# Products with v in one group per head: an order of work rearranged in a kernel for hashed attention and soft mixture of experts

## The chip, the core and the metric

The kernel runs on one core of one Trainium2 chip. A core has five engines that each work through their own instructions in the order in which the program wrote them: TensorE (PE in the profile; PEld is its loading of weights), VectorE (DVE), ScalarE (ACT), GpSimd (POOL) and SyncE (SP), which here only issues transfers. The metric is the time of one execution on the device in microseconds (us), lower is better. Times are medians of several runs; a profile comes from one execution.

## What is computed

There are 4 batches of 8 heads, 768 positions, 64 dimensions a head.

```python
q_bits = (np.einsum('bhsd,dk->bhsk', q, proj) > 0)      # 6 bits, and the same for k
mask = q_bucket[:, :, :, None] == k_bucket[:, :, None, :]
scores = scale * np.matmul(q, k.transpose(0, 1, 3, 2))
scores = np.where(mask, scores, -1000000000.0)
scores = scores - np.max(scores, axis=-1, keepdims=True)
attn = np.exp(scores)
attn = attn / (np.sum(attn, axis=-1, keepdims=True) + 1e-09)
attn_out = np.matmul(attn, v)
...
x = attn_out.transpose(0, 2, 1, 3).reshape(3072, 512)
logits = x @ phi                                        # 32 slots
d = softmax of logits over the 3072 rows; slot_input = d.T @ x
h = np.maximum(slot_input[e] @ w1[e], 0.0); slot_out[e] = h @ w2[e]   # 8 experts
c = softmax of logits over the 32 slots; return c @ slot_out
```

## The kernel before, in words

Heads are worked on in pairs, an even one and the odd one behind it, because q and k of two heads fill the 128 partitions together. Four things overlap: loading and splitting the next pair, the maxima of the next head, the scores of this head, and the sums of the last pair.

For a pair, `bits` (line 322) multiplies q and k with the projection on TensorE, in column tiles of 32 (several small products side by side in the array), and VectorE thresholds the result (line 319) into `bt`. ScalarE writes rounded high parts of q and k into `w4` (`split_hi`, line 279), and `split_lo` (line 288) subtracts them from the originals to get the low parts. The `spread` functions copy all this into the operands X and Y of the two heads, by transfers that SyncE issues from line 294.

For a head, `smax` (line 358) makes the masked scores once in order to take the row maxima: 12 calls, in PSUM tiles of which there are two, each emptied by a VectorE reduction (lines 371 and 374). `shift` (line 376, VectorE) turns the maxima into a shift, and `shift_rows` (line 387) transposes it on TensorE (line 402), copies it on ScalarE (line 405) and sends it into a row of X and Y. `scores` (line 409) makes the scores a second time, now shifted, transposed, in full-width matmuls (line 419), and ScalarE takes the exponential into the three buffers `pts` (line 423). Each of the buffers holds two of a head's six row tiles. `acc` (line 425) adds a buffer into a running sum on GpSimd (lines 430, 436), `av` (line 438) multiplies it with v on TensorE in two column tiles of 64 (line 447). The third `av` of a head is followed by a copy on ScalarE (line 451, `avs`).

For a pair that is through, `pair_sum` (line 454) adds the partitions of the running sums on TensorE in column tiles of 32 (line 459), and ScalarE copies the result to `sm` (line 462). `pair_log` (line 468) multiplies the heads' outputs with phi in row and column tiles (line 474). `pair_turn` (line 490) transposes the sums (line 494), after which VectorE copies and inverts them (lines 496, 497), `pair_rec` (line 464) inverts `sm` in three pieces on VectorE (line 466), `pair_add` (line 478) adds the scaled logits into `lacc` (lines 486, 488), and `pair_x` (line 499) transposes the outputs and scales them into `xq` (lines 509, 511).

At the end of a batch, `batch_max` and the functions behind it fold the logits' halves together (lines 605, 606, VectorE), take maxima and exponentials, transpose them (line 636), multiply them with `xq` (line 653) and rescale the running results. The experts' layers come after all heads.

The order is written by hand. `WHEN` gives each call a due time in slots (six slots a head), `FIRST` overrides single calls, `at` collects them, and the plan is sorted by due time; the calls are then made in that order, and every engine gets its instructions in that order. A call of two engines (a matmul and the reduction of its result) stands at the same place in both. Waits are semaphores put in for the buffers and operands. `p_mi`, the PSUM pool of the sums, logits, bits and transposes, has two tiles, the pool of the scores has three, `raw`, `w4` and `bt` have one each.

In an even head the order around line 494 is, before: the turn, two of the reciprocals, av 1 and the logits, the first scores of the odd head, a maximum, av 2.

Of the kernel before, what the change touches and what calls it, by code (L numbers as in the profile page):

```python
# [12 lines left out]
ALU = mybir.AluOpType  # L13
# [32 lines left out]
 'bits': -14.465,  # L46
 'split_hi': -14.035,
 'split_lo': [-13.1, -12.626],
# [19 lines left out]
 'batch_scale': 24.396,  # L68
 'batch_slots': 26.173,
 'batch_combine': 24.296,  # L70
 'load_weights': 4.18}

FIRST = {('load', 4): 4.476,
 ('bits', 2): 1.288,
# [71 lines left out]
def lsh_attention_soft_moe(  # L146
# [141 lines left out]
    def split_lo(h, x):  # L288
        w = st[h]["w4"]
        (nc.vector if h else nc.gpsimd).tensor_tensor(out=w[:, 2 * x + 1], in0=st[h]["raw"][:, x], in1=w[:, 2 * x], op=ALU.subtract)  # L290
# [308 lines left out]

    def batch_max(b):  # L600
        z = bst[b]
        if "dl" not in z:
            lacc = lacc_of[b]
            dl = z["dl"] = dp.tile([P, HC], F32, name="dl", bufs=1)
            nc.vector.tensor_copy(dl[0:64], lacc[64:128])
            nc.vector.tensor_tensor(out=dl[64:128], in0=lacc[0:64], in1=dl[0:64], op=ALU.add)  # L606
# [16 lines left out]
    def batch_scale(b):  # L623
        z = bst[b]
        if b == 0:
            nc.vector.tensor_copy(run_l, z["lb"])
        else:
            nc.vector.tensor_copy(z["al"][64:128], z["al"][0:64])
            nc.vector.scalar_tensor_tensor(out=run_l, in0=run_l, scalar=z["al"][0:2 * NS], in1=z["lb"],
                                           op0=ALU.mult, op1=ALU.add)  # L630
# [55 lines left out]
    def batch_combine(b):  # L686
        z = bst[b]
        lg = z["tm"][:, :, 1]
        m = dp.tile([P, 3, 2], F32, name="cm", bufs=1)
        sm = dp.tile([P, 3, 2], F32, name="cs", bufs=1)  # L690
        cb = call[:, b]
        nc.vector.tensor_reduce(out=m, in_=lg, axis=AX.X, op=ALU.max)
        nc.vector.tensor_tensor(out=cb, in0=lg, in1=m[:, :, :, None].broadcast_to([P, 3, 2, NS]), op=ALU.subtract)
        nc.scalar.activation(cb, cb, AF.Exp)
# [3 lines left out]
        nc.vector.tensor_tensor(out=cb, in0=cb, in1=sm[:, :, :, None].broadcast_to([P, 3, 2, NS]), op=ALU.mult)  # L698
# [17 lines left out]
    for h in range(BH):  # L716
# [16 lines left out]
        for j in range(NT // 2):  # L733
# [5 lines left out]
            else:  # L739
                at(s0 + WHEN["av"][x][j], av, h, j)  # L740
# [10 lines left out]
        if h % H == H - 1 and h < BH - 1:  # L751
            for f in (batch_max, batch_exp, batch_turn, batch_scale, batch_slots, batch_combine):
                at(p0 + WHEN[f.__name__], f, h // H)
# [72 lines left out]
    batch_combine(B - 1)  # L826
# [170 lines left out]
```

## Time and profile before

| | |
|---|---|
| median of 3 runs | 537.56 us (537.41 to 540.1) |
| the profiled execution | 537.24 us |
| its span from first to last instruction | 535.4 us |
| granted TensorE clock, mean | 0.972 |
| busy: PE, PEld | 503.6, 286.7 us |
| busy: DVE, ACT, POOL | 388.9, 246.6, 317.9 us |
| instructions | 9102 |

An engine's busy time is the time in which it worked on some instruction. In the rows of the profile an operation is named by its engine, its line in the kernel, what it writes and reads, its shape, and how often it came. "L368 <- DVE mx L374" behind a time says that the instruction waited that long and that the named one ended the wait. Matmuls are pipelined: the next one starts before the recorded end of the last, so distances between starts tell more than durations.

### The profile page before, as it was taken

What the parts mean: (1) busy time and instruction counts of PE and PEld (TensorE: products, weight loads), DVE (VectorE), ACT (ScalarE), POOL (GpSimd) and SP (SyncE); (2) the same over time, 40 slices, a digit from 0 to 9 for tenths busy, and PEclk for the clock granted to TensorE, in tenths of its full rate; (3) what the DMA queues carried; (4) which work ended last, traced back from release to release, by engine and by line L of the source; (5) the groups of instructions that cost most, each with busy time, mean ns of one, the idle gap of its engine ahead of it and who ended that gap; (6) DMA issues with size and microseconds to landing.
All of it is one profiled execution on the core that took longest, in us unless ns stands there. A gap on an engine that the chain in (4) does not pass through costs nothing.

```text
span 535.4 us, 9102 instructions
## 1 busy us (share of the span) xinstructions
PE 503.6 (94%) x3164; PEld 286.7 (54%) x3164; DVE 388.9 (73%) x717; ACT 246.6 (46%) x460; POOL 317.9 (59%) x210
## 2 busy tenths in 40 slices
PE   6979999999989999999989999999899999999992
PEld 4544555655545565656544555565445656553562
DVE  6475777888898777877898788686997875465233
ACT  4145455545453454545453545454534555422232
POOL 9256858585854576767646585858635767511200
PEclk9789999999998999999989999999999999999997
DMA  4766566757673667676753757676626366888976
GB/s 123 184 137 152 173 174 187 186 174 183 175 179 95 177 180 180 179 178 178 185 163 98 184 176 179 187 180 190 130 76 144 77 150 217 296 314 330 409 284 275
DMA packets 39778, 99.60 MB, mean 186 GB/s; under 512 B 7458, under 2 KB 13732, under 8 KB 39732
## 3 DMA queue, kind: packets, MB, share of 16 engines
q1 hardware_dynamic: 39540, 98.94, 64.7%
q8 instruction: 25, 0.41, 0.3%
q14 instruction: 21, 0.17, 0.1%
q0 software_dynamic: 192, 0.08, 0.1%
HBM read 52.76 MB, written 6.29 MB: 110 GB/s over the span
## 4 chain that ended last, share of the span: by engine, by line
PE 71%; DVE 17%; DMA 4%; SPq 3%; issue 2%; ACT 1%; DVEq 0%; ACTq 0%
PE av L447 20%; PE st L419 20%; PE smx L368 12%; DVE mx L374 4%; DVE w L290 4%; SPq L294 3%; PE qs L920 3%; PE qh L838 3%; PE mi L459 2%; PE mi L474 2%; DVE mx L371 2%; PE mi L326 1%; DVE dl L606 1%; DMA XY<-bt 1%; DMA XY<-mr 1%
## 5 line engine op out<-in xcount | busy, mean ns | idle before, releaser
L436 POOL TENSOR_TENSOR acc<-acc,pt 128x768 f32<-128x768 f32 x125 | 236.4, 1891 | 56.2 <-ACT pt L423 45.8
L423 ACT ACTIVATE pt<-st 128x512 f32<-128x512 f32 x288 | 163.1, 595 | 105.1 <-PE st L419 98.2
L419 PE MATMUL st<-XY 128*128 128x512 f32 (+1 forms) x768 | 184.1, 348 | 0.0
L374 DVE TENSOR_REDUCE mx<-smx 128x1 f32<-128x512 f32 x192 | 130.4, 686 | 56.2 <-PE smx L368 55.9
L447 PE MATMUL av<-pt,v 128*64 128x384 f32 x768 | 148.4, 508 | 0.0
L368 PE MATMUL smx<-XY 96*128 96x512 f32 (+1 forms) x384 | 127.3, 378 | 18.0 <-DVE mx L374 14.5
L419 PEld LDWEIGHTS st<-XY 128*128 128x128 f32 x768 | 123.9, 191 | 21.2 <-issue 10.6
L430 POOL TENSOR_TENSOR acc<-pt 128x768 f32<-128x768 f32 x32 | 58.5, 1829 | 98.0 <-ACT pt L423 98.0
L368 PEld LDWEIGHTS smx<-XY 96*128 96x128 f32 x384 | 71.2, 193 | 81.1 <-DVE mx L374 35.9
L447 PEld LDWEIGHTS av<-pt,v 128*64 128x64 f32 x768 | 47.0, 137 | 63.2 <-issue 57.2
L371 DVE TENSOR_REDUCE mx<-smx 128x2 f32<-128x512 f32 x96 | 65.5, 682 | 4.8 <-PE smx L368 4.6
L290 DVE TENSOR_TENSOR w<-raw,w 128x768 fp32r<-128x768 f32 x30 | 41.3, 1377 | 2.9 <-ACT w L286 2.8
L466 DVE RECIPROCAL sm<-sm 128x128 f32<-128x128 f32 x45 | 39.6, 909 | 0.0
L286 ACT CAST w<-raw 128x768 fp32r<-128x768 f32 x32 | 25.1, 830 | 18.6 <-DMA XY<-w 14.1
L451 ACT COPY avs<-av 128x384 f32<-128x384 f32 x32 | 15.3, 479 | 37.3 <-PE av L447 37.2
L405 ACT CAST mr<-mi 12x128 fp32r<-12x128 f32 x31 | 7.9, 254 | 51.1 <-PE mi L402 51.1
L319 DVE TENSOR_SCALAR bt<-mi,con 128x384 fp32r<-128x384 f32 x15 | 10.1, 677 | 18.4 <-PE mi L402 8.8
L511 DVE TENSOR_TENSOR xq<-mi,r 128x256 f32<-128x256 f32 x45 | 17.3, 412 | 0.4 <-PE mi L509 0.4
L920 PE MATMUL qs<-w 128*32 128x256 f32 x232 | 15.2, 382 | 0.0
L509 PE MATMUL mi<-ident,avs 128*128 128x128 f32 x90 | 14.8, 273 | 0.0
L326 PE MATMUL mi<-raw,pb 128*32 128x384 f32 x128 | 14.5, 498 | 0.3 <-DMA raw<-qk 0.2
L838 PE MATMUL qh<-w,siT 128*32 128x512 f32 x128 | 14.6, 595 | 0.0
(169 smaller groups left out, 340.7 us busy)
## 6 DMA issues: line engine op xcount, KB each, us to landing
w<-w SPq DMA_DIRECT2D x61, 512.0 KB
XY<-w SPq DMA_DIRECT2D x63, 384.0 KB
raw<-qk SPq DMA_DIRECT2D x32, 384.0 KB
XY<-w SPq DMA_DIRECT2D x64, 192.0 KB
v<-vt SPq DMA_DIRECT2D x32, 192.0 KB
out<-w SPq DMA_DIRECT2D x12, 512.0 KB
xq<-w SPq DMA_DIRECT2D x3, 512.0 KB
XY<-bt SPq DMA_DIRECT2D x62, 19.5 KB
```

What stands on the lines that cost most here:

```text
L290: (nc.vector if h else nc.gpsimd).tensor_tensor(out=w[:, 2 * x + 1], in0=st[h]["raw"][:, x], in1=w[:, 2 * x], op=ALU.subtract)
L368: nc.tensor.matmul(pt[:, o:o + b - a], s["Y"][0:96, 0, t * P:(t + 1) * P], s["Y"][0:96, 1, a:b], start=True, stop=True)
L371: nc.vector.tensor_reduce(out=mx[:, n - 1:n + 1], in_=pt.rearrange("p (a x) -> p a x", a=2), axis=AX.X, op=ALU.max)
L374: nc.vector.reduce_max(out=mx[:, n:n + 1], in_=pt, axis=AX.X)
L419: nc.tensor.matmul(pt[:, o:o + b - a], x[:, 1, i * P:(i + 1) * P], x[:, 0, a:b], start=first, stop=not first)
L423: nc.scalar.activation(s["P", i // 2][:, 512 * u:512 * u + 512], pt, AF.Exp, scale=D ** -0.5)
L430: nc.gpsimd.tensor_tensor(out=s["acc"], in0=pr[:, 0:S], in1=pr[:, S:2 * S], op=ALU.add)
L436: eng.tensor_tensor(out=s["acc"], in0=s["acc"], in1=pr[:, a * S:(a + 1) * S], op=ALU.add)
L447: nc.tensor.matmul(s["av"][64 * c:64 * c + 64, 0:HC], s["v"][:, i, :], pr[:, o + c * HC:o + (c + 1) * HC], start=(i == 0), stop=(i == NT - 1))
L466: nc.vector.reciprocal(out=rs[:, k * P:(k + 1) * P], in_=rs[:, k * P:(k + 1) * P])
L838: nc.tensor.matmul(ph[fh][32 * j:32 * j + 32], siT[:, k, 4 * g + j, :], wt[0, g, k, j][:, fh * 512:(fh + 1) * 512], start=(k == 0), stop=( ...
L920: nc.tensor.matmul(po[32 * j:32 * j + 32], hTs[g][:, f, 32 * j:32 * j + 32], wt[1, x, 2 * g + f // 4, j][:, (f % 4) * HM:(f % 4 + 1) * HM] ...
```

## The change

No product is added or left out. The due times move, three VectorE steps move to other engines, and two functions are cut in two. In short:

- the three `av` calls of a head stand together behind its last scores; for an even head `pair_sum` and `pair_log` stand ahead of them and `pair_turn` and two pieces of `pair_rec` behind them; for an odd head `bits` stands behind them, `split_hi` and both `split_lo` between them
- `shift_rows` moves later, `pair_x` earlier
- `split_lo` of q runs on GpSimd for all pairs (before: for the first pair alone)
- the fold of the logits' halves becomes `batch_both`, with the copy on ScalarE and the addition on GpSimd, at 20.1 instead of 21.535
- the update of `run_l` and two steps of the combination weights run on GpSimd, for all batches but the last
- the last head's `av` and the first pair's start keep their old times

```diff
- 'bits': -14.465,
- 'split_hi': -14.035,
- 'split_lo': [-13.1, -12.626],
+ 'bits': -12.18,
+ 'split_hi': -12.196,
+ 'split_lo': [-12.193, -12.19],
- 'shift_rows': [-2.151, -1.917],
+ 'shift_rows': [-1.8, -1.1],
- 'av': [[3.513, 6.554, 6.938], [3.513, 5.087, 6.68]],
- 'pair_sum': 16.448,
- 'pair_turn': 18.256,
- 'pair_rec': [18.379, 18.389, 18.942],
- 'pair_log': 18.557,
- 'pair_x': [22.815, 24.33],
+ 'av': [[6.7, 6.71, 6.72], [5.8, 5.81, 5.82]],
+ 'pair_sum': 18.6,
+ 'pair_turn': 18.74,
+ 'pair_rec': [18.75, 18.76, 18.942],
+ 'pair_log': 18.65,
+ 'pair_x': [22.3, 23.0],
- 'batch_max': 21.535,
- 'batch_exp': 22.897,
- 'batch_turn': 23.51,
+ 'batch_both': 20.1,
+ 'batch_max': 22.4,
+ 'batch_exp': 23.0,
+ 'batch_turn': 23.9,
- 'batch_combine': 24.296,
+ 'batch_weigh': 24.65,
+ 'batch_share': 27.6,
...
-        (nc.vector if h else nc.gpsimd).tensor_tensor(out=w[:, 2 * x + 1], ...
+        (nc.vector if h and x else nc.gpsimd).tensor_tensor(out=w[:, 2 * x + 1], ...
...
+    def batch_both(b):
+        lacc = lacc_of[b]
+        dl = bst[b]["dl"] = dp.tile([P, HC], F32, name="dl", bufs=1)
+        nc.scalar.copy(dl[0:64], lacc[64:128])
+        nc.gpsimd.tensor_tensor(out=dl[64:128], in0=lacc[0:64], in1=dl[0:64], op=ALU.add)
...
-            nc.vector.tensor_copy(dl[0:64], lacc[64:128])
-            nc.vector.tensor_tensor(out=dl[64:128], in0=lacc[0:64], in1=dl[0:64], op=ALU.add)
...
+            if b < B - 1:
+                nc.gpsimd.tensor_tensor(out=run_l, in0=run_l, in1=z["al"][0:2 * NS], op=ALU.mult)
+                nc.gpsimd.tensor_tensor(out=run_l, in0=run_l, in1=z["lb"], op=ALU.add)
...
+    def batch_weigh(b):
...
+        eng = nc.gpsimd if b < B - 1 else nc.vector
+        nc.vector.tensor_reduce(out=m, in_=lg, axis=AX.X, op=ALU.max)
+        eng.tensor_tensor(out=cb, in0=lg, in1=m[...].broadcast_to([P, 3, 2, NS]), op=ALU.subtract)
+        nc.scalar.activation(cb, cb, AF.Exp)
+    def batch_share(b):
...
+        nc.vector.reciprocal(out=sm, in_=sm)
+        eng.tensor_tensor(out=cb, in0=cb, in1=sm[...].broadcast_to([P, 3, 2, NS]), op=ALU.mult)
```

More of the change, by code (lines that the diff above doesn't have):

```diff
@@ L289, in split_lo @@
         w = st[h]["w4"]
-        (nc.vector if h else nc.gpsimd).tensor_tensor(out=w[:, 2 * x + 1], in0=st[h]["raw"][:, x], in1=w[:, 2 * x], op=ALU.subtract)
+        (nc.vector if h and x else nc.gpsimd).tensor_tensor(out=w[:, 2 * x + 1], in0=st[h]["raw"][:, x], in1=w[:, 2 * x], op=ALU.subtract)
     def move(dst, src, eng=nc.sync):
@@ L697, in batch_combine @@
         nc.vector.reciprocal(out=sm, in_=sm)
-        nc.vector.tensor_tensor(out=cb, in0=cb, in1=sm[:, :, :, None].broadcast_to([P, 3, 2, NS]), op=ALU.mult)
+        eng.tensor_tensor(out=cb, in0=cb, in1=sm[:, :, :, None].broadcast_to([P, 3, 2, NS]), op=ALU.mult)
     plan = []
@@ L751, in lsh_attention_soft_moe @@
         if h % H == H - 1 and h < BH - 1:
[L752 removed]
+            for f in (batch_both, batch_max, batch_exp, batch_turn, batch_scale, batch_slots, batch_weigh, batch_share):
                 at(p0 + WHEN[f.__name__], f, h // H)
```

28 lines of the change are left out of this document (15 added, 13 removed).

## The prediction

> **What bounds the kernel now.** I read the page first: busy shares, then the chain that ended last.
>
> ```profile
> PE 503.6 (94%) x3164; PEld 286.7 (54%) x3164; DVE 388.9 (73%) x717; ACT 246.6 (46%) x460; POOL 317.9 (59%) x210
> PE 71%; DVE 17%; DMA 4%; SPq 3%; issue 2%; ACT 1%; DVEq 0%; ACTq 0%
> ```
>
> TensorE is busy nearly always, and the chain runs through it; VectorE holds most of the rest. These are averages, so next came the busy time by stretches, each from one pair's sums (line 459) to the next pair's. Columns: length, then busy time of PE, weight loads, DVE, ACT, POOL, and the granted clock.
>
> ```profile
> 254.20:288.80 34.60, 30.70 (x171) 16.65 (x170) 31.49 (x52) 15.38 (x30) 19.39 (x12) 0.95 0.53 139
> 315.40:341.60 26.20, 26.20 (x156) 15.18 (x155) 20.16 (x39) 13.70 (x25) 19.16 (x11) 1.00 0.67 183
> ```
>
> In an ordinary pair TensorE never stops: 26.20 of 26.20 us. A pair with a batch end takes 8.4 us more. So an ordinary pair can only gain if its TensorE work gets cheaper, and any new wait of TensorE adds in full.
>
> **What a group costs.** The timeline of TensorE around one set of products with v, asked in narrow slices so that each start can be read (start, time, operation; a row can run on into the next):
>
> ```profile
> 312.20 0.40 PE L419 MATMUL st<-XY 128*128 128x512 f32 x1
> 312.43 0.39 PE L419 MATMUL st<-XY 128*128 128x512 f32 x1
> 312.75 0.54 PE L447 MATMUL av<-pt,v 128*64 128x384 f32 x2
> 313.12 0.81 PE L447 MATMUL av<-pt,v 128*64 128x384 f32 x4
> 313.77 0.49 PE L447 MATMUL av<-pt,v 128*64 128x384 f32 x2
> 314.19 0.50 PE L368 MATMUL smx<-XY 96*128 96x512 f32 x1
> 314.53 0.28 PE L402 MATMUL mi<-ident,mz 128*12 128x128 f32 x1
> ```
>
> Two 512-column matmuls start 0.23 apart; the second is followed after 0.32 when the tiling changes (+0.09). Two column halves take (313.77 - 313.12) / 2 = 0.325, the first 0.37 (+0.045), the last 0.42 (+0.095); the first full-width matmul afterwards takes 0.34 instead of 0.23 (+0.11). One excursion into column tiles costs 0.34 us.
>
> Before, a pair makes seven: the even head's av 0; the sums; av 1 with the logits; av 2; the odd head's av 0 with the bits; av 1; av 2. After, it makes two: sums, logits, av 0, 1, 2; and av 0, 1, 2, bits. Five fewer save 5 x 0.34 = 1.7; one more change of form inside a group returns about 0.1. **-1.6 us a pair, -24 us over 15 pairs.** The Trainium skill, "TensorEngine Tiling (Array Packing)", section Key Properties, says that changing the tiling mode drains TensorE; the rows above price that drain. By the rule alone the change would be a plain gain, which is the first rival below.
>
> **What the long groups do to VectorE.** TensorE obeys the written order, and so does VectorE. Before, TensorE's order around the turn of the sums (line 494) is:
>
> ```profile
> 317.97 0.49 PE L494 MATMUL mi<-ident,sm 128*128 128x128 f32 x3
> 318.39 1.51 PE L447 MATMUL av<-pt,v 128*64 128x384 f32 x8
> 319.83 0.85 PE L474 MATMUL mi<-avs,phs 64*32 64x384 f32 x8
> 320.61 0.73 PE L419 MATMUL st<-XY 128*128 128x512 f32 x2
> 323.29 0.63 PE L419 MATMUL st<-XY 128*128 128x256 f32 x4
> 323.77 0.28 PE L368 MATMUL smx<-XY 96*128 96x256 f32 x1
> ```
>
> and VectorE's, in the same microseconds:
>
> ```profile
> 319.14 0.16 DVE L496 COPY r<-mi 128x12 f32<-128x12 f32 x1
> 319.34 0.23 DVE L497 RECIPROCAL r<-r 128x12 f32<-128x12 f32 x1
> 319.48 1.71 DVE L466 RECIPROCAL sm<-sm 128x128 f32<-128x128 f32 x2
> 321.62 0.69 DVE L374 TENSOR_REDUCE mx<-smx 128x1 f32<-128x512 f32 x1 [0.43 <-PE smx L368]
> 322.23 0.94 DVE L466 RECIPROCAL sm<-sm 128x128 f32<-128x128 f32 x1
> 324.10 0.55 DVE L486 TENSOR_TENSOR sm<-mi,sm 128x384 f32<-128x384 f32 x1
> 324.68 0.56 DVE L488 TENSOR_TENSOR lacc<-lacc,sm 128x384 f32<-128x384 f32 x1
> 325.16 0.68 DVE L371 TENSOR_REDUCE mx<-smx 128x2 f32<-128x512 f32 x1
> 325.84 0.69 DVE L374 TENSOR_REDUCE mx<-smx 128x1 f32<-128x512 f32 x1
> 326.57 0.17 DVE L380 TENSOR_REDUCE m<-mx 128x6 f32<-128x12 f32 x1
> 326.77 0.38 DVE L381 TENSOR_SCALAR mz<-m 128x6 f32<-128x6 f32 x1
> 327.18 0.17 DVE L383 SCALAR_TENSOR_TENSOR mz<-m,mz 128x6 f32<-128x6 f32 x1
> ```
>
> The two reciprocals run while TensorE does av 1 and the logits, 2.22 us in which it needs nothing of VectorE. Starts follow at 0.61 after a reduction, 0.81 a reciprocal (half of 1.71 with overlap), 0.20 and 0.14 for the two small ones, 0.58 and 0.48 for the additions, 0.68 and 0.73 for the last reductions.
>
> After, the turn comes *behind* the whole group, and VectorE's queue holds the copy of r, hence everything later, until then. Count from the start of the turn. It ends at about 0.6; r's copy starts at 0.65, its reciprocal at 0.85, the long ones at 0.99 and 1.80, the next reduction of the maxima at 2.61, ending at 3.30. TensorE meanwhile does the turn (0.43), one score pair of 512 (2 x 0.23), two maxima of 512 (0.47) and two score pairs of 256 (4 x 0.12), and at 1.85 wants a PSUM buffer for the next maxima. There are two, and that reduction holds one: TensorE stands 1.5 us. VectorE stays the late one: third reciprocal 3.22, reduction 4.03, additions 4.64 and 5.22, reductions 5.70 and 6.38, then the shift (lines 380 to 383) 7.10 to 7.88. The row of shifts (line 402) needs it. Without waits TensorE would be there after five score pairs of 512 (2.34), five of 256 (1.2), four maxima of 512 (0.93), two of 256 (0.24) and the turn: 5.14. **First window: +2.75 us.** Line 381 can also take longer, as here:
>
> ```profile
> 286.63 1.03 DVE L381 TENSOR_SCALAR mz<-m 128x6 f32<-128x6 f32 x1
> ```
>
> Ends: 2.0, if of the waits behind the first 1.5 only half a microsecond is real; 3.4, if line 381 takes its 1.03 each time. A gain is excluded, since nothing leaves VectorE's queue in this window. I take 2.75, every term of which has a row.
>
> **Second window**, behind the odd group, with the bits at its end:
>
> ```profile
> 328.85 0.68 DVE L319 TENSOR_SCALAR bt<-mi,con 128x384 fp32r<-128x384 f32 x1 [1.50 <-PE mi L402]
> 332.50 3.57 SPq L294 DMA_DIRECT2D XY<-bt  x4
> 126.16 2.27 DMA XY<-bt
> ```
>
> VectorE now thresholds the bits (0.68) just as the window opens and its maxima queue behind: TensorE waits 0.5 and 0.1 for buffers. Then the next even head's first maxima need the bits' four rows. The threshold ends at 0.83, the last of four issues starts 3/4 x 3.57 later, and it lands 2.27 after that: 5.8. TensorE would be there at 4.35 (four score pairs of 512, four of 256, four maxima of 512, four of 256, first matmul +0.1): 1.45 late, the 0.6 included. Before, the four issues start at 332.50 in a pair that ends at 341.60, with these maxima among its last work. Another 0.25 goes on the maxima that wait behind the shift. **Second window: +1.7 us** (0.6 if only the buffers count, 2.2 if SyncE's queue is late). Nothing gives these back: the groups last about 5.5 and 4.9 us, and VectorE has only two buffered reductions to do in each.
>
> Every full pair has both windows: 14 x 4.45 = **+62 us**. The last pair has no maxima left.
>
> **Moves that cost nothing or little.** The prices of q's low part on the two engines, and of a sum on GpSimd:
>
> ```profile
> L290 POOL TENSOR_TENSOR w<-raw,w 128x768 fp32r<-128x768 f32 x2 | 3.7, 1856 | 0.1
> L290 DVE TENSOR_TENSOR w<-raw,w 128x768 fp32r<-128x768 f32 x30 | 41.3, 1377 | 2.9 <-ACT w L286 2.8
> L436 POOL TENSOR_TENSOR acc<-acc,pt 128x768 f32<-128x768 f32 x125 | 236.4, 1891 | 56.2 <-ACT pt L423 45.8
> ```
>
> GpSimd gets 1.86 more beside its 19.16 in 26.20, and holds the odd head's second and third accumulation until ScalarE's casts are done, beside av 0. From the start of the 4.9 us group they end after about 1.2 (the last exponential and a cast, an estimate) + 1.86 + 4 x 1.89 = 10.6, 5.7 into the second window; the exponentials that need the buffer follow the maxima that wait until 5.8, at about 6.6. If that cover is gone, each microsecond beyond delays the row of shifts. VectorE loses 1.38, but out of a time when it would be idle (the odd group), so I give it nothing; ScalarE's casts too move there and cost nothing. SyncE's queue gets the copies of the low parts later and, behind GpSimd's subtraction, the next load of q and k; their first readers come a head later or more, so half a pair, 13 us, hides this. The row of shifts goes out later with its copy, but a group of about 5 us lies between it and the scores that read it. The turns of xq move ahead of the odd group; they are the same six transposes, and their multiplications come last in the first window's queue, with the group behind them, which needs nothing of VectorE. "GPSIMD Engine Reference", section 8 Key points, of the Trainium skill warns that GpSimd contends with a VectorE instruction that has two SBUF inputs. The spread of line 290 fits it; here the odd group hides what remains.
>
> **Batch ends** (three).
>
> ```profile
> 268.09 2.08 DVE L606 TENSOR_TENSOR dl<-lacc,dl 64x384 f32<-64x384 f32 x1
> 272.40 0.50 PE L368 MATMUL smx<-XY 96*128 96x512 f32 x1 [2.57 <-DVE mx L374]
> 273.90:277.20 3.30, 3.30 (x12) 1.81 (x9) 3.30 (x3) 0.79 (x2) 1.38 (x1) 0.50 0.36 77
> ```
>
> Two copies of this length leave VectorE; the 2.57 wait and the half clock after it (1.65 us of work lost in 3.30) can go. The two additions to the running sum and two steps of the combine go to GpSimd as well. But GpSimd's new addition stands ahead of the even head's last accumulation and waits for the logits (5.8 in the first window) and a ScalarE copy. With about 0.95 for it (half of 1891) and two accumulations of 1.89 the buffer frees near 11; the row's cast and the turn of xq queue behind that exponential, a new wait of about 2.6. Each end can bring -4.2 (both waits go) to +1 (the new one is longer); I take -1.65, the half clock alone, since the 2.57 comes back in another place: **-5 us** in all.
>
> **Sum.** All waits of the maxima for a reduction, in the list of waits (total, count, longest):
>
> ```profile
> PE smx L368 <- DVE mx L374: 14.5, 13, 2.9
> ```
>
> The profiled execution took 537.24 (span 535.4 and 1.8 around it), 0.3 under the median of 537.56. 537.2 - 24 + 62 - 5 - 1 (an estimate for the short ones of these waits) = **569 us**.
>
> **Rivals.** (1) *The drains decide*: VectorE keeps up, and only the saving is left: 537 - 24 - 1 - 5 = 507. For it: VectorE idles 6 us in a pair. Against: the idle time moves into the groups, where nothing is ready for it. It turns on the stall per pair: under (24 + 5 + 1) / 14 = 2.1 us the change wins. 0.10. (2) *Half the stalls*: 30 back for 30 saved, 537 or no change, 0.04. (3) *The clock also falls*: a 2.57 wait halved it above; if 2.75 us of waits in one window do the same each time, 14 x 1.65 = 23 more, 592. The 1.5 piece alone may not do it. 0.10. The Trainium skill, "TensorE: Matmul & The Clock Gate", section Why this matters for your kernels, puts the limit at gaps over about 3 us; the row at 273.90 shows the half clock after 2.57 already, so the measurement decides. (4) *My own forecast*, 0.76.
>
> **Range.** The bounds of the two windows, 2.6 to 5.6 us a pair, give 36 to 78 us for 14, the batch ends -13 to +3; all low at once is 535, all high 591, where rival 3 ends too. The low corner needs every bound together and goes out with rivals 1 and 2: 543 to 592. A measurement of this kernel can tell about 0.5% from no change. Chances: faster 0.10, same 0.04, slower 0.86.
>
> **What would show it.** Right: two excursions into column tiles a pair, a pair period near 29, the wait of line 368 for line 374 grown from 14.5 to over 35 us, line 402 waiting for line 383, line 368 for the bits' copies, and a lower busy share of TensorE. Wrong: no idle time before line 368 behind the turn, a pair period near 24.6, or GpSimd's accumulations as the releaser of line 423.

## The result, and the profile after

The changed kernel takes 614.46 us (median of 4 runs, 610.88 to 619.12), the kernel before 537.48 on the same chip: 1.144 times as long, 95% interval 1.134 to 1.154. The forecast of 569 had the sign and less than half of the size: +31 against +77. The changed kernel has seven more lines ahead of all that matters here, so line 368 of before is line 375 now, 374 is 381, 383 is 390, 402 is 409, 423 is 430, 488 is 495, and so on. Where the runs of one kernel lie more than 1.5% apart, as those of the three joins below do, its ratio is taken from the shorter ones.

The page of the changed kernel, busy shares, granted clock by slices, and the chain:

```profile
PE 517.9 (85%) x3164; PEld 309.4 (51%) x3164; DVE 385.3 (63%) x688; ACT 247.5 (41%) x463; POOL 352.6 (58%) x238
...
PEclk9879898989899999988899989899798999999997
...
PE 51%; DVE 30%; POOL 7%; DMA 4%; issue 3%; ACT 2%; SPq 1%; DVEq 0%; ACTq 0%; POOLq 0%
```

TensorE's share of the chain went from 71% to 51%, VectorE's from 17% to 30%, and GpSimd has appeared on it. The granted clock is below 9 tenths in 14 of the 40 slices.

Next the 14 full pairs as one stretch, from the first pair's sums (line 459, now 466) to the fifteenth's. Columns: length, busy time of PE, weight loads, DVE, ACT, POOL, granted clock. First before, then after with two single pairs:

```profile
61.98:453.21 391.23, 379.30 (x2205) 216.35 (x2204) 315.60 (x548) 195.51 (x362) 262.51 (x141) 0.99 0.62 165
```

```profile
67.08:529.36 462.28, 393.27 (x2201) 235.83 (x2200) 309.19 (x519) 195.57 (x364) 291.30 (x166) 0.95 0.55 139
201.64:231.86 30.22, 26.11 (x157) 15.92 (x156) 21.25 (x36) 13.35 (x25) 20.96 (x12) 1.00 0.53 138
264.89:300.50 35.61, 29.77 (x156) 18.34 (x156) 23.54 (x37) 13.91 (x25) 20.98 (x12) 0.88 0.54 138
```

The pairs grew by 462.28 - 391.23 = 71.1 us, nearly all of the loss; 5.1 more came ahead of them (67.08 against 61.98), with 4.4 us more of idle TensorE there, which was not followed up. TensorE's idle time rose from 391.23 - 379.30 = 11.9 to 462.28 - 393.27 = 69.0, by **57 us**. Its busy time rose by 14.0, and the clock alone would make it more: a twentieth of 393.27 less a hundredth of 379.30 is **16 us** (the two digits leave about 3). The trace has 13 half-clock stretches in the 14 pairs, 3 before; half of the busy time in them (47.0 and 10.2) gives 18. So busy time at full clock fell by 2 to 4 us only, although five of seven excursions into column tiles are gone; "The drains by themselves" has the reason.

The mean pair period, batch ends included, is 462.28 / 14 = 33.0, and was 27.9.

**Where TensorE waits.** The list of waits (total, count, longest):

```profile
PE smx L375 <- DVE mx L381: 38.9, 29, 2.1
...
PE smx L375 <- DVE mx L378: 12.0, 19, 1.5
...
PE smx L375 <- DMA XY<-bt: 7.5, 10, 0.9
...
PE mi L409 <- DVE mz L390: 4.3, 12, 0.6
```

Buffers of the maxima that VectorE has not emptied, the bits' copies, the row of shifts: the waits that the prediction named. In the timeline they can be timed. TensorE, first in the pair at 201.64, where the turn of the sums starts at 207.23, then in the pair at 264.89, where it starts at 271.13:

```profile
203.20 4.09 PE L454 MATMUL av<-pt,v 128*64 128x384 f32 x24
207.23 0.55 PE L501 MATMUL mi<-ident,sm 128*128 128x128 f32 x3
...
210.47 0.39 PE L375 MATMUL smx<-XY 96*128 96x256 f32 x1 [1.27 <-DVE mx L381]
...
214.23 0.28 PE L409 MATMUL mi<-ident,mz 128*12 128x128 f32 x1 [0.23 <-DVE mz L390]
...
216.94 0.54 PE L454 MATMUL av<-pt,v 128*64 128x384 f32 x2
...
225.72 0.63 PE L426 MATMUL st<-XY 128*128 128x512 f32 x2
227.57 0.70 PE L375 MATMUL smx<-XY 96*128 96x512 f32 x3 [1.22 <-DVE mz L388]
...
271.13 0.55 PE L501 MATMUL mi<-ident,sm 128*128 128x128 f32 x3
...
274.38 0.39 PE L375 MATMUL smx<-XY 96*128 96x256 f32 x1 [1.27 <-DVE mx L381]
...
278.91 0.50 PE L375 MATMUL smx<-XY 96*128 96x512 f32 x1 [1.48 <-DVE mx L378]
...
280.12 0.38 PE L409 MATMUL mi<-ident,mz 128*12 128x128 f32 x1 [0.46 <-DVE mz L390]
...
283.92 0.54 PE L454 MATMUL av<-pt,v 128*64 128x384 f32 x2
```

The first wait ends 3.24 and 3.25 us behind the start of the turn. The prediction's count gives 1.85 + 1.5 = 3.35. The row of shifts comes 7.00 behind it in the first of the two pairs, which opens a batch and so has one addition less, and 8.99 in the second; the count gives 7.88. The window up to the next group lasts 9.71 in the one and 12.79 in the other. What lengthens the second, an addition of 2.05 instead of 0.56, a further wait of 1.48 and a slower clock, was not in the forecast.

**Who makes the further waits.** VectorE's and GpSimd's timelines at those places:

```profile
227.51 1.74 DVE L390 SCALAR_TENSOR_TENSOR mz<-m,mz 128x6 f32<-128x6 f32 x1
...
276.21 2.05 DVE L495 TENSOR_TENSOR lacc<-lacc,sm 128x384 f32<-128x384 f32 x1
```

```profile
227.41 1.82 POOL L437 TENSOR_TENSOR acc<-pt 128x768 f32<-128x768 f32 x1
...
249.60 1.82 POOL L297 TENSOR_TENSOR w<-raw,w 128x768 fp32r<-128x768 f32 x1 [5.46 <-ACT w L293]
251.39 8.26 POOL L443 TENSOR_TENSOR acc<-acc,pt 128x768 f32<-128x768 f32 x4
259.61 1.81 POOL L437 TENSOR_TENSOR acc<-pt 128x768 f32<-128x768 f32 x1
261.50 7.49 POOL L443 TENSOR_TENSOR acc<-acc,pt 128x768 f32<-128x768 f32 x4
...
276.01 1.83 POOL L437 TENSOR_TENSOR acc<-pt 128x768 f32<-128x768 f32 x1 [7.02 <-ACT pt L430]
```

Line 390 works on 6 elements a partition and takes 0.17 us in the prediction's row. Here it starts at 227.51, 0.1 behind a GpSimd sum, and ends at 229.25, when that sum ends (227.41 + 1.82 = 229.23). Line 495 starts 0.2 behind another and ends 0.4 after it, 2.05 instead of 0.56. Both read two operands from SBUF, the memory that the engines share. The middle rows show how the collisions come about: GpSimd waits 5.46 for ScalarE's cast, takes q's low part and then has no gap from 249.60 to 269.0, which covers VectorE's next shift (line 390 at 259.71 takes 1.73 and ends with the sum of 259.61). 11 of the 32 instructions of line 390 are that long, all 0.1 behind the start of a head's first GpSimd sum, and 7 of the 11 of line 495 are held up by one too. In the list by lines and shapes (busy, mean ns) the two groups read

```profile
L390 DVE SCALAR_TENSOR_TENSOR mz<-m,mz 128x6 f32<-128x6 f32 x32 | 23.3, 727 | 1.1
...
L495 DVE TENSOR_TENSOR lacc<-lacc,sm 128x384 f32<-128x384 f32 x11 | 15.4, 1401 | 0.4
```

At the durations of before they would take 32 x 0.17 = 5.4 and 11 x 0.56 = 6.2: **27 us** more on VectorE, in the queue that TensorE waits for. The third kind with two SBUF operands, k's low part (line 297), rose from a mean of 1377 to 1890 ns, 7.7 us for its 15, so that taking 15 of the 30 low parts off VectorE relieved it by 41.3 - 28.4 = 12.9 us only. The Trainium skill, "SBUF — State Buffer", section Who interferes with whom, says that a VectorE instruction with two SBUF inputs contends with a GpSimd instruction that reads SBUF. The trace agrees, and its price here is up to the whole of a sum, 1.8 us.

**How the clock falls.** The half-clock stretches in this trace are 3.41 us long, or twice that, and start on one grid of that step. Consecutive grid steps of the changed kernel, in the columns of the windows view:

```profile
242.48:245.89 3.41, 1.93 (x9) 1.19 (x8) 3.34 (x5) 1.91 (x4) 1.66 (x1) 1.00 0.49 190
245.89:249.31 3.42, 2.78 (x18) 2.04 (x19) 3.02 (x9) 1.85 (x4) 0.00 (x0) 1.00 0.01 2
259.55:262.96 3.41, 1.75 (x11) 1.24 (x10) 3.38 (x5) 0.60 (x1) 3.33 (x3) 1.00 1.01 317
262.96:266.38 3.42, 3.42 (x19) 1.67 (x21) 1.66 (x3) 1.45 (x3) 3.26 (x3) 0.50 1.04 284
```

A step with 1.48 us of idle TensorE (3.41 - 1.93) is followed by full clock, a step with 1.66 (3.41 - 1.75) by half clock. No single wait need be long: in the version at 547.95 below, the step from 247.82 has 1.38 us of idle time in three waits of at most 0.56, and half clock follows, while the 1.48 above is one wait. What counts is their sum in one step, and so where the steps happen to fall.

### The profile page after: what moved, and what is told of

It is laid out like the page before. It is cut to its first block, busy times and chain, and to the rows that moved or that the text cites. A ratio compares the mean times of both kernels' runs of the same rounds, so it can differ in the third digit from the quotient of the medians.

```text
span 610.9 us, 9137 instructions
## 1 busy us (share of the span) xinstructions
PE 517.9 (85%) x3164; PEld 309.4 (51%) x3164; DVE 385.3 (63%) x688; ACT 247.5 (41%) x463; POOL 352.6 (58%) x238
## 4 chain that ended last, share of the span: by engine, by line
PE 51%; DVE 30%; POOL 7%; DMA 4%; issue 3%; ACT 2%; SPq 1%; DVEq 0%; ACTq 0%; POOLq 0%
PE av L454 17%; PE st L426 10%; PE smx L375 7%; DVE mx L381 7%; DVE sm L473 5%; POOL acc L443 5%; DVE mx L378 5%; DVE mz L390 3%; PE qs L938 2%; PE mi L466 2%; DMA XY<-mr 2%; PE qh L856 2%; DVE lacc L495 2%; PE mi L481 2%; DVE mz L388 2%
## 5 line engine op out<-in xcount | busy, mean ns | idle before, releaser
L426 PE MATMUL st<-XY 128*128 128x512 f32 (+1 forms) x768 | 190.6, 363 | 8.8 <-ACT pt L430 4.8
L375 PE MATMUL smx<-XY 96*128 96x512 f32 (+1 forms) x384 | 132.5, 397 | 65.5 <-DVE mx L381 38.9
L426 PEld LDWEIGHTS st<-XY 128*128 128x128 f32 x768 | 131.5, 203 | 34.4 <-issue 11.0
L454 PE MATMUL av<-pt,v 128*64 128x384 f32 x768 | 131.4, 491 | 0.0
L375 PEld LDWEIGHTS smx<-XY 96*128 96x128 f32 x384 | 76.7, 206 | 105.0 <-DVE mx L381 52.1
L437 POOL TENSOR_TENSOR acc<-pt 128x768 f32<-128x768 f32 x32 | 59.1, 1846 | 80.2 <-ACT pt L430 75.5
L454 PEld LDWEIGHTS av<-pt,v 128*64 128x64 f32 x768 | 52.1, 137 | 72.5 <-issue 72.2
L378 DVE TENSOR_REDUCE mx<-smx 128x2 f32<-128x512 f32 x96 | 65.6, 683 | 12.9 <-PE smx L375 12.8
L297 POOL TENSOR_TENSOR w<-raw,w 128x768 fp32r<-128x768 f32 x17 | 31.0, 1822 | 64.6 <-ACT w L293 64.5
L297 DVE TENSOR_TENSOR w<-raw,w 128x768 fp32r<-128x768 f32 x15 | 28.4, 1890 | 9.7 <-ACT w L293 9.1
L612 POOL TENSOR_TENSOR dl<-lacc,dl 64x384 f32<-64x384 f32 x3 | 3.0, 998 | 38.0 <-ACT dl L611 38.0
L390 DVE SCALAR_TENSOR_TENSOR mz<-m,mz 128x6 f32<-128x6 f32 x32 | 23.3, 727 | 1.1
L326 DVE TENSOR_SCALAR bt<-mi,con 128x384 fp32r<-128x384 f32 x15 | 10.1, 675 | 20.4 <-DMA XY<-w 12.9
```

The costliest lines, as they stand in the source:

```text
L297: (nc.vector if h and x else nc.gpsimd).tensor_tensor(out=w[:, 2 * x + 1], in0=st[h]["raw"][:, x], in1=w[:, 2 * x], op=ALU.subtract)
L375: nc.tensor.matmul(pt[:, o:o + b - a], s["Y"][0:96, 0, t * P:(t + 1) * P], s["Y"][0:96, 1, a:b], start=True, stop=True)
L378: nc.vector.tensor_reduce(out=mx[:, n - 1:n + 1], in_=pt.rearrange("p (a x) -> p a x", a=2), axis=AX.X, op=ALU.max)
L390: nc.vector.scalar_tensor_tensor(out=mz[:, 0:NT], in0=m, scalar=-1.0, in1=mz[:, NT:2 * NT], op0=ALU.mult, op1=ALU.subtract)
L426: nc.tensor.matmul(pt[:, o:o + b - a], x[:, 1, i * P:(i + 1) * P], x[:, 0, a:b], start=first, stop=not first)
L437: nc.gpsimd.tensor_tensor(out=s["acc"], in0=pr[:, 0:S], in1=pr[:, S:2 * S], op=ALU.add)
```

## The experiments

Theory A, formed on these rows: the stalls of the prediction are real, and two things come on top of them, GpSimd's instructions that hold up VectorE's, and the clock. Rival B: the stalls follow from the order of VectorE's queue alone, and were only mis-sized. Rival C: the drains are not what they seemed, and regrouping saves nothing. The recorded expectations use other letters: their theory Q is B, their theory G the GpSimd part of A and their theory C its clock part; D and H concern the batch ends alone. Times are medians; ratios, with 95% intervals, are to the kernel before on the same chip, which took 537.3 to 538.3 us in all of these runs.

### Undoing the change step by step

The sums and their turn early again:

```diff
- 'pair_sum': 18.6, 'pair_turn': 18.74, 'pair_rec': [18.75, 18.76, 18.942],
+ 'pair_sum': 16.448, 'pair_turn': 18.256, 'pair_rec': [18.379, 18.389, 18.942],
```

> The changed kernel, with the sums, their turn and the first two reciprocals back at their old due times, ahead of the even head's group; the products with v, the logits and everything else stay in the new order. Theory Q (VectorE's queue stands behind the turn): the 1.3 us wait of the maxima behind the turn and the 1.5 us one after it disappear in all 15 pairs, one more excursion into column tiles costs 0.34, and with the waits most of the half-clock stretches of the first window go: 614 falls by 45 to 60, to 555-570. Theory G (GpSimd's dense stretch slows VectorE): the waits only shrink by what VectorE's load falls, 605 or more.

**576.48 us**, 1.073 [1.068, 1.077]: 38 us less, with the low part of q still on GpSimd, between the two ranges that were expected and nearer to B's. The wait of line 375 for line 381 falls from 38.9 to 11.2 us, while lines 390 and 495 stay as long (23.4 and 16.4 in total). In this order of undoing, the turn behind the long group is the largest step.

On top of it the bits, casts and low parts at their old times:

```diff
- 'bits': -12.18, 'split_hi': -12.196, 'split_lo': [-12.193, -12.19],
+ 'bits': -14.465, 'split_hi': -14.035, 'split_lo': [-13.1, -12.626],
```

> The changed kernel with the turn early (576) and the bits, ScalarE's casts and both low parts at their old due times too; q's low part stays on GpSimd. If the bits behind the odd group cost the 0.7 us wait for their copies and the crowding of VectorE's queue behind it, 15 pairs x 1 to 1.5 go, and one more excursion costs 0.3 a pair: 558-566. If the bits' place was free, the extra excursion makes it 578-582.

**547.86**, 1.018 [1.014, 1.021]: another 29 less, more than expected.

On top of that, q's low part on VectorE again:

```diff
- (nc.vector if h and x else nc.gpsimd).tensor_tensor(...)
+ (nc.vector if h else nc.gpsimd).tensor_tensor(...)
```

> The same version as the first of this call with full sums (547.86 us), and q's low part on VectorE again. This is then the batch-end version (523.66 us) with the products with v, sums and logits in groups, the shift's rows later and the turns of xq earlier. If q's low part made the 24 us between the two: near 525 us, and with the drains' saving down to 510. If the group of products itself makes them: 540 to 550 us.

**547.95**, 1.020 [1.017, 1.024]: no difference. What is left against before is the group of products and logits (the sums stand alone again), later rows of shifts and earlier turns of xq, and the batch-end steps, which alone gain 14 (below). So the first three together lose 24 us, with fewer excursions; no run takes the rows of shifts or the turns of xq back alone. The list by shapes and the timelines of this kernel show part of what eats the saving:

```profile
L495 DVE TENSOR_TENSOR lacc<-lacc,sm 128x384 f32<-128x384 f32 x11 | 16.4, 1491 | 0.4
```

```profile
216.73 1.83 POOL L437 TENSOR_TENSOR acc<-pt 128x768 f32<-128x768 f32 x1 [4.11 <-ACT pt L430]
...
216.96 2.02 DVE L495 TENSOR_TENSOR lacc<-lacc,sm 128x384 f32<-128x384 f32 x1
...
219.63 0.50 PE L375 MATMUL smx<-XY 96*128 96x512 f32 x1 [0.48 <-DVE mx L378]
...
220.94 0.28 PE L409 MATMUL mi<-ident,mz 128*12 128x128 f32 x1 [0.56 <-DVE mz L390]
...
221.73 0.66 PE L516 MATMUL mi<-ident,avs 128*128 128x128 f32 x4 [0.40 <-DVE bt L326]
```

The addition of line 495 starts 0.2 behind a GpSimd sum and ends 0.4 after it, although within a pair nothing is on GpSimd that was not there before: the grouping has moved VectorE's queue and GpSimd's sums, which follow the exponentials, against each other. The waits of the row of shifts, and of the turns of xq for the bits' threshold, come right behind; the latter wait, 3.1 us in 9 pieces over the whole kernel, belongs to the turns' earlier place. The low parts, both on VectorE here, take 55.2 us against 41.4 in the kernel with the batch-end steps alone (523.66, below).

### q's low part

In the changed kernel back on VectorE (the same edit as above, nothing else):

> The changed kernel, with q's low part back on VectorE for all pairs but the first; nothing else. Theory G: GpSimd's accumulations no longer stand behind the subtraction that waits for ScalarE's cast, they spread out, and VectorE's two-input steps (line 390, mean 727 ns, line 495, mean 1401 ns) fall back to near 170 and 580 ns: 25 to 35 us less, 580-590. Theory Q: VectorE's queue behind the turn and the bits is as long as before, 0 to 10 us less, 604-614.

**597.87**, 1.110 [1.103, 1.117]: 17 us of the loss go, between the two ranges that were expected. Line 390 falls from 23.3 to 9.3 us in total, line 495 from 15.4 to 12.4.

Both this and the early turn:

> The changed kernel with both earlier edits: the sums and their turn early, q's low part back on VectorE. If the two causes add, 614 - 38 - 17 = 559; what is then left over 537 less the batch ends is the bits' place. If GpSimd's accumulations decide behind the first window too, the two overlap and it stays at 565-576.

**587.6**, 1.095 [1.088, 1.102], above both ranges that were expected. Steps of 38 and 17 together give 27: with the turn early, q's low part on VectorE *costs* 11 us. The waits of the two kernels, first with the early turn alone, then with both, show one that grew:

```profile
PE st L426 <- DMA XY<-mr: 6.5, 7, 2.0
```

```profile
PE st L426 <- DMA XY<-mr: 19.9, 9, 3.8
```

The row of shifts lands late: VectorE now has both low parts between the maxima. Which of its instructions delays the row most was not tried.

The reverse test, the kernel before with the batch-end steps alone (523.66, below) and q's low part on GpSimd at its old place:

> The kernel before with the batch-end steps alone (523.66 us), and q's low part on GpSimd for all pairs at its old place in the order. If the low part is dear on GpSimd wherever it stands (1.86 us more a pair on an engine that VectorE's additions wait for): 8 us or more slower, 532 to 545 us. If it was dear only where it stood in the changed kernel, behind the casts and bunched with the accumulations: within 3 us of 523.7.

**532.66**, 0.991 [0.988, 0.994]: 9 us dearer, as the first expectation has it, but not because additions wait: the additions and the shift's last step take what they took without it (6.4 and 6.0 us in total). What grew is the shift's middle step (line 381 of before, one SBUF operand), from 10.7 to 17.9 us, and k's low part, to a mean of 1690 ns. So the step is worth -17, +11, 0 and +9 us by what stands around it (back to VectorE in the first three, to GpSimd in the last). It has no price of its own; by these rows it hangs on which VectorE instructions GpSimd's work then meets.

### GpSimd's load taken away

Four of GpSimd's five sums of a head on 32 columns instead of 768, which leaves out most of the row sums, in the changed kernel and, as a control, in the kernel before (the expectations count by the six row tiles; the first sum adds two):

```diff
- eng.tensor_tensor(out=s["acc"], in0=s["acc"], in1=pr[:, a * S:(a + 1) * S], op=ALU.add)
+ m = S if h >= BH - 2 else 32
+ eng.tensor_tensor(out=s["acc"][:, 0:m], in0=s["acc"][:, 0:m], in1=pr[:, a * S:a * S + m], op=ALU.add)
```

> The changed kernel, with GpSimd's second to sixth accumulation of a head done on 32 columns instead of 768 (heads 0 to 29), so that most of the row sums are left out and the result is not the reference's; the number and the order of the instructions are the same. GpSimd is then almost free. Theory Q (VectorE's own queue and the bits' place, without GpSimd): about the sum that the prediction made for them, 14 x 4.45 of waits less the drains, 565 to 585. Theory G: with GpSimd out of the way VectorE's two-input steps take 0.17 and 0.56 again and the waits mostly go, 520-545.

> The kernel before with the same shortened accumulations, as the control: its ordinary pairs have no wait that GpSimd ends, so only the batch ends can gain (the fold's two steps of 1.9 and 2.1 us become 0.4 and 0.6): 525-535.

**579.34**, 1.077 [1.074, 1.080], and **521.08**, 0.969 [0.965, 0.972]. The load costs 35 us in the changed kernel and 17 in the kernel before, more there than was expected. The control was needed: of the change's loss GpSimd's load makes about 18 us by these two runs, not 35. In the changed kernel line 390 is near its old duration again, which alone is 23.3 - 6.0 = 17 us less on VectorE; the addition (here line 496) is not, since it meets the one long sum that was left:

```profile
L496 DVE TENSOR_TENSOR lacc<-lacc,sm 128x384 f32<-128x384 f32 x11 | 15.4, 1400 | 0.4
...
L390 DVE SCALAR_TENSOR_TENSOR mz<-m,mz 128x6 f32<-128x6 f32 x32 | 6.0, 187 | 1.1
```

So 58 us remain above the control: the order of VectorE's queue, as B has it, the addition's 9 us and the clock (7 half-clock stretches in the pairs, none in the control; about 12 us). Neither theory is enough alone. The same cut in the version with turn and bits at their old times:

> The version with the turn early and bits, casts and low parts at their old places (547.86 us), with GpSimd's second to sixth accumulation of a head on 32 instead of 768 columns; the row sums are left out. The control is the kernel before with the same cut, 521.08 us. If GpSimd's load is what eats the drains' saving here: the control less four excursions (7 to 3 a pair) at about 0.29 us over 15 pairs, 17 us: 500 to 510 us, clearly below the control. If the grouped av and the order of VectorE's work lose the time by themselves: near 535 us or more, and above the control.

**531.41**, 0.989 [0.986, 0.992]: 16 less than with full sums, and still 10 above the control, between the two outcomes that were expected. (The expectation counts three excursions left; the timeline has four, since the sums too stand alone again.) The 14 pairs in the windows view, first of this kernel, then of the control:

```profile
61.41:448.06 386.65, 375.62 (x2206) 223.54 (x2205) 273.61 (x520) 194.15 (x365) 117.18 (x165) 1.00 0.66 168
```

```profile
61.64:439.22 377.58, 373.37 (x2205) 213.54 (x2204) 289.99 (x548) 195.67 (x362) 86.04 (x139) 1.00 0.66 171
```

At full clock and with GpSimd nearly out of the way, this version adds 6.8 us of idle time (11.0 against 4.2) and saves nothing of the busy time. This is C's outcome, but not for C's reason, as the next section shows.

### The drains by themselves

The kernel before, with av 2 of the even head directly behind av 1 and the logits, one excursion less:

```diff
- 'av': [[3.513, 6.554, 6.938], [3.513, 5.087, 6.68]],
+ 'av': [[3.513, 6.554, 6.56], [3.513, 5.087, 6.68]],
```

> The kernel before, with one edit: the even head's third product with v is put directly behind its second and the logits, so that each pair makes six excursions into column tiles instead of seven. VectorE has two reciprocals and then a third to do in that stretch and nothing there needs TensorE. If an excursion costs 0.34 us as the rows said: 15 x 0.34 = 5 us less, 532. If joined groups always bring a wait of VectorE's queue: no change or up to 10 us more.

**545.55**, 1.016 [1.013, 1.019]: slower by 8. Its wait for the row of shifts, its additions as a group, then TensorE, VectorE and GpSimd in one of its pairs:

```profile
PE mi L402 <- DVE mz L383: 11.9, 13, 1.8
...
L488 DVE TENSOR_TENSOR lacc<-lacc,sm 128x384 f32<-128x384 f32 x11 | 21.1, 1917 | 0.4
...
243.08 0.28 PE L402 MATMUL mi<-ident,mz 128*12 128x128 f32 x1 [1.01 <-DVE mz L383]
...
239.10 2.02 DVE L488 TENSOR_TENSOR lacc<-lacc,sm 128x384 f32<-128x384 f32 x1
...
238.87 1.83 POOL L430 TENSOR_TENSOR acc<-pt 128x768 f32<-128x768 f32 x1 [3.69 <-ACT pt L423]
```

Moving 1.4 us of TensorE's work forward was enough to bring the addition of line 488 into the head's first GpSimd sum: 2.02 instead of 0.56, and the row of shifts waits 1.01 for what follows it. All 11 additions are that long, 21.1 us in total against 6.4 before, and the waits for the row rose from 1.1 to 11.9.

The price of the drain itself holds, and the saving is there. In the changed kernel 24 products with v take 207.23 - 203.20 = 4.03 us; the row of before at 318.39 has 8 in 1.44, three times 4.32. The 0.29 saved are the parts inside the group of two excursions, 2 x (0.045 + 0.095), as the prediction had them. The rest shows when the distances between the starts of TensorE's instructions in the 14 pairs are sorted by kind, recorded idle time taken off and half-clock time counted half. The rows into, inside and out of column tiles take 178.2 us before and 156.5 after: 22 less, and 14 x 1.6 = 22.4 was forecast.

But a wait costs more than the list of waits says. A 512-column matmul is recorded with 0.40 although the next can start after 0.23, so the first 0.17 of a wait behind it look busy; and the matmul that comes after a wait keeps its successor 0.10 longer than others do. In the changed kernel 90 matmuls ahead of a wait and 70 behind one take 21 us that way, before 0.7. So the waits grew by 57 + 21 = 78 us, and their hidden part ate what the drains saved. In the version at 531.41 it is the same: 13.5 us less than the control in and around column tiles, 16 more around waits.

Two more joins, with the batch-end steps:

```diff
- 'av': [[3.513, 6.554, 6.938], [3.513, 5.087, 6.68]], 'pair_sum': 16.448,
+ 'av': [[3.513, 6.554, 6.56], [3.513, 6.67, 6.68]], 'pair_sum': 15.515,
...
```

> The kernel before with the batch-end steps moved and three joins that leave the turn of the sums, the bits and q's low part at their old places: the sums behind the even head's first product with v, its third product behind the second, and the odd head's second and third together. Four excursions a pair instead of seven: 15 x 1.0 = 15 us and 5 for the batch ends, 517 if VectorE has no more to do behind these groups than it can; if the longer group of the odd head starves it as in the changed kernel, 525 to 540.

**556.9** (547.19 to 559.23), 1.025 [1.016, 1.034]. A miss: even the shortest of its runs lies above both ranges that were expected, and above the 532.18 of the same batch-end steps without the joins (below). In neither test did fewer drains make this kernel faster; which wait makes the loss of the three joins was not followed up.

### The clock

To keep TensorE busy without changing any order, idle products of the unit matrix with itself stand ahead of the maxima that wait, from the fifth head on:

```diff
+    def fill(n):
...
+        for _ in range(n):
+            nc.tensor.matmul(pt[:, 0:P], ident, ident, start=True, stop=True)
```

> The changed kernel, with idle-time matmuls of an identity (5 to 13 of them, full width, into the free bank of the products with v) ahead of the four maxima on which TensorE waits longest; they leave the results alone. Theory C (the waits also halve the clock, some 15 stretches of 3.4 us at half speed against 3): the clock stays at 1.0 through the pairs and the time falls by 15 to 25, to 590-600, while the waits stay where they are. If the clock is only a by-product, the fillers cost up to a few microseconds: 612-620.

**639.54**, 1.191 [1.185, 1.196]. Too much filling: each call came out as two matmuls, so the blocks were longer than the waits.

```profile
256.75 2.84 PE L261 MATMUL av<-ident 128*128 128x128 f32 x24
```

Half as many:

> The changed kernel with the idle-time matmuls of the identity again, half as many calls (each call turned out as two matmuls of 0.11 us, so the earlier fillers were longer than the waits they were to fill). Now they are as long as the waits: 2, 6, 5 calls in an even head and 6 in an odd one. Theory C: the clock stays up in the pairs, the waits for VectorE stay as they are, and the time falls by the half-clock loss beyond that of before, 15 to 20 us, to 594-600. If the clock were only a by-product the time would stay at 612-618.

**598.81**, 1.114 [1.108, 1.119]. The 14 pairs:

```profile
66.60:511.95 445.35, 426.94 (x2717) 285.24 (x2717) 307.25 (x519) 194.87 (x365) 293.07 (x166) 1.00 0.57 144
```

The clock is whole (1.00), and the kernel takes 15.7 us less although TensorE does 516 matmuls more in these pairs. That agrees with the 16 to 18 us from the changed kernel's own clock, which costs at least the 15.7, since some of the filling may still be longer than the wait that it fills.

### The batch ends alone

The kernel before with nothing but the batch-end steps on ScalarE and GpSimd, the first at the time that the change gives it, the others at the old ones; then all of them at the change's later times:

```diff
- 'batch_max': 21.535, 'batch_exp': 22.897, 'batch_turn': 23.51, 'batch_combine': 24.296,
+ 'batch_both': 20.1, 'batch_max': 21.535, 'batch_exp': 22.897, 'batch_turn': 23.51, 'batch_weigh': 24.296, 'batch_share': 24.297,
...
```

> The kernel before, with only the batch-end steps moved off VectorE (the fold of the logits on ScalarE and GpSimd, the running sum and two steps of the combination on GpSimd, the fold issued at 20.1), all other due times old. Theory D (the fold was late work on VectorE): the three 2.57 us waits and their half clock go, 5 to 13 us less, 525-532. Theory H (GpSimd in order holds the accumulation behind the fold): the new wait takes its place, 535-540.

```diff
+ 'batch_both': 20.1, 'batch_max': 22.4, 'batch_exp': 23.0, 'batch_turn': 23.9, 'batch_weigh': 24.65, 'batch_share': 27.6,
...
```

> The kernel before with the batch-end steps moved off VectorE (532) and issued at the later due times of the changed kernel, the last steps of the combination last. If the waits of 1.2 us before the turn of the batch's logits and of 1.7 us for the next shift came from steps issued before their inputs were there, 3 to 6 us less than the early order: 526-529. If not: 531-535.

**532.18**, 0.990 [0.985, 0.996], and **523.66**, 0.974 [0.970, 0.977]: this one, faster than was expected, beats both kernels, by 2.6% and 15%. A pair with a batch end and its neighbour, in the windows view:

```profile
250.17:279.55 29.38, 29.09 (x172) 15.65 (x171) 23.43 (x46) 15.40 (x31) 19.23 (x15) 1.00 0.63 164
279.55:306.01 26.46, 26.37 (x156) 15.19 (x155) 20.86 (x37) 13.71 (x25) 21.48 (x12) 1.00 0.67 181
```

The batch end costs 29.38 - 26.46 = 2.9 us more than an ordinary pair; before it cost 8.4. VectorE's busy time in it fell from 31.49 to 23.43, idle time from 3.90 to 0.29, and the clock stays whole. The later times matter as much as the other engines: at the old ones TensorE still waits, at the later ones it finds the results there.

## Why the prediction was right in sign and wrong in size

**Right: the waits by name.** The named signs are there: the waits of line 375 for line 381 at 38.9 us (over 35 was said), line 409 waiting for line 390, line 375 for the bits' copies, a lower TensorE share. The first wait was counted to end at 3.35 us behind the turn and ends at 3.25. The 10 waits for the bits' copies average 0.75; the count had 1.45 - 0.6 = 0.85. In the undoing, the turn is worth 38 us and the bits, casts and low parts 29; the two windows were put at 14 x 2.75 = 38.5 and 14 x 1.7 = 23.8. Part of that agreement is chance: the undoing also took contention and clock away, which were not in those two terms. The pair period, put near 29, is missed: 30.2 and 35.6 in the two pairs shown, 33.0 in the mean.

**Right: the drains, -24.** The distances between starts show 22 us less in 14 pairs. It can't be seen in the busy time, since the waits hide as much in rows that look busy.

**Wrong: "VectorE loses 1.38 ... so I give it nothing" and "here the odd group hides what remains".** This step priced GpSimd's work by GpSimd's own time and by who waits for its results. It left out whom GpSimd holds up. VectorE's durations were copied from rows of before, where no GpSimd sum held up line 383 (all 32 at 0.17) and hardly one the additions (a median of 0.56, one at 0.81), and used unchanged in a new order. Lines 390 and 495 took 27 us more. The 1.38 has contention in it already: 21 of the 30 low parts of before took 0.96 or less, the others up to 2.58. By the runs with short sums, 35 - 17 = 18 us of the loss are GpSimd's load, part of them through the clock. The failure is not q's low part alone, whose place on GpSimd cost 17, -11, 0 and 9 us by its surroundings; a new order moves GpSimd's sums, which follow the exponentials, over other VectorE instructions, as the single join shows with nothing moved to GpSimd at all.

**Wrong: the clock as a rival at 0.10.** Its price was near (23 us forecast, 16 to 18 measured), its chance was not. "The 1.5 piece alone may not do it" looked at single waits; in a grid step of 3.41 us they add up. Contention is not needed for all of it: with GpSimd's sums cut short there are still 7 half-clock stretches in the pairs, against 13. The Trainium skill, "TensorE: Matmul & The Clock Gate", section What's actually happening, describes a free-running window of 3413 ns, which the grid agrees with; its idle window is not needed here, since 1.66 us of idle time in a step sufficed.

**Wrong: the batch ends, -5.** The range was -13 to +3 and the runs give -14 on the kernel before: I took the half clock alone, on the ground that the 2.57 us come back in another place. That is what the steps give at the old times (-5, with waits left); at the later times, which the change has, both waits went, and the "new wait of about 2.6" did not come. What they are worth inside the changed kernel no run separates. (What leaves VectorE is one copy of 1.88 and the addition of 2.08, not two copies.)

Summed up: recorded waits +57, their hidden part +21, drains -22, clock +16 to 18, ahead of the pairs +5 give 77 to 79, against 610.9 - 535.4 = 75.5 between the two profiled executions. The forecast had +61 for the waits (62 - 1), -24 for the drains, -5 for the half clock at the batch ends and nothing ahead of the pairs. So two steps failed: the waits came out 17 longer than counted, with VectorE's durations taken over unchanged as one cause, and the clock, which was to give back 5, cost 16 or more. How the 17 divide between contention and mis-sized windows stays open, since the batch-end waits, whose gain nothing separates here, are in the same sum. In the range, the upper corner adds up to 593 and not 591 (537.2 - 24 + 78 + 3 - 1); no conclusion turns on it.

## What to carry to other kernels

When an order is rearranged, list for every VectorE instruction with two SBUF operands which GpSimd instruction runs beside it before and after; a tiny one on the path can cost a whole GpSimd instruction. Sum TensorE's expected waits over any stretch of 3.4 us, not one by one, before calling them harmless to the clock. And cut a change into its parts: here one part was worth -2.6% and was buried under three others.

## What the runs showed of the hardware

- The clock follows the sum of idle time on a fixed grid of 3.41 us. In the changed kernel every full-clock step inside the pairs with 1.52 us or more of recorded idle TensorE was followed by half clock, and none with 1.48 or less; in the other kernels the edge lay between 1.38 and 1.74.
- A VectorE instruction with two SBUF inputs that started just behind a GpSimd sum was held up until the sum ended: 0.17 became 1.74, 0.56 became 2.05. One input can be enough: 18 of the 32 instructions of line 381 in the kernel before (a tensor_scalar of 6 columns, 0.17 to 0.27 otherwise) started behind a GpSimd sum and ended just after it, most at 0.38, the longest at 1.42.
- A wait of TensorE cost about 0.17 us ahead of it and 0.10 behind it more than the recorded idle time: 21 us for the 90 and 70 matmuls of the changed kernel's pairs.
- A product of two 128-column fp32 operands came out as two matmuls of about 0.11 us each between starts, 2.84 for 24 in the row above, so the first filling had twice the matmuls that its calls suggest.
